# Attention prologue reordered: mask fill by token halves, layer norm of x in pairs, more v products before the first logits, four rotating PSUM banks

## The chip, the core and the metric

One core of one Trainium2 chip. TensorE is PE here, its weight loads PEld; VectorE is DVE, ScalarE ACT, GpSimd POOL, SyncE SP. DMAs are issued from the queues of SP, ACT and POOL, in the order in which those engines run their programs. The metric is the device time of one execution in microseconds, lower is better.

## The reference, cut to what matters

```python
def _A_ref(x, wqkv, wo):                      # B, S, D = 1, 2048, 576; H = 32 heads, Dh = 18
    qkv = (x @ wqkv).reshape(B, S, 3, H, Dh).transpose(2, 0, 3, 1, 4)
    q, k, v = qkv
    idx = pos[:, None] - (jnp.arange(8) * 2)[None, :]      # window of 8 keys, two tokens apart
    logits = einsum('bhsd,bhswd->bhsw', q, k[idx]) * Dh ** -0.5
    logits = where(idx >= 0, logits, -1e9)
    attn = softmax(logits)
    return einsum('bhsw,bhswd->bhsd', attn, v[idx]) (heads joined) @ wo

def _B_ref(x, w_in, w_sp, b_sp, w_out):       # F = 4608, gated with a 2048 x 2048 matrix over tokens
    z = gelu(x @ w_in); z1, z2 = halves of z; z2 = layernorm(z2)
    return (z1 * (w_sp @ z2 + b_sp)) @ w_out

x = x + _A_ref(layernorm(x), ...)             # layer 0
x = x + _B_ref(layernorm(x), ...)             # layer 1
x = x + _A_ref(layernorm(x), ...)             # layer 2
x = x + _B_ref(layernorm(x), ...)             # layer 3
```

## The kernel before, in words

The four layers run one after the other. The change touches the two attention layers (`layer_A`, li 0 and 2), above all what comes before their first logits. Inside `layer_A` the order of PE, ACT, DVE, POOL and SP is the order in which the program is written: each engine runs its instructions in that order, and so does each DMA queue.

**Layer norm and transposes of x (layer 0).** x is 16 tiles of 128 tokens. Statistics are three DVE instructions a tile (`LNX_stats`, L501 and L502), then epsilon is added (L504), POOL takes the power -1/2 (L505, called R here), and DVE applies it (L513). Tiles 0 to 3 are transposed on PE into `xnT` and copied by ACT (L520); tiles 4 to 15 by DMA transposes on SP (`ln_T`, L245). Statistics go by 2, 2, 2, 2, 4 and 4 tiles.

**Mask rows.** `QK` holds for each head 18 rows of q (index 0) and k (index 1) and 14 rows of a pattern that yields the window mask in the logits product: 128 partitions, four heads each, by 8 groups g of heads by 16 + 2048 tokens. `fill_window_rows` copies a pattern of 256 columns into all of it with DVE (L185, L187, L189), by pairs of groups.

**q and k (PG).** `PG(d, qk, cc)` is five matmuls (L383): seven heads (d = 0 to 3; four for d = 4), q or k, 512 tokens (cc). PSUM is copied to a staging tile `stg` by ACT (L355) or DVE (L353). When a staging tile is full (1024 tokens, q and k), one DMA for each head copies its 18 rows into `QK` (QK<-stg), dealt to the queues of POOL and SP by a fixed pattern (`queues`, 2 to 1). There are three staging tiles in layer 0, four in layer 2. Twenty PGs (cc = 0 and 1) come before the logits and four more (`pgs[:4]`) follow; 16 are spread over the steps.

**v (VW).** `VW(t, hh)` is five matmuls (L361) and one copy into `v_ext`, 19 columns a head, the last of which is 1. Six VW stand early in layer 0, two in layer 2; the others are spread over the steps.

**Steps.** Queries go in 19 tiles t of 112 tokens, each in two halves of 16 heads: step s = 2t + hf, 38 steps. Step s runs the logits of step s + 1 (`L_mm`, L407), the exponentials of s + 1 on ACT (`EXP`, L416), then PV(s) (L427) and DVE's division (L433, L434). After the second half the result is transposed into `oT` by a DMA on SP (L438). Logits need heads 0 to 15 in even steps, 16 to 31 in odd ones. A hand-written `table` adds to step s: PGs up to step 13 (`PG_END` = 14), VW(t) at 2t - 2 and 2t - 1, output projections `WO(i, hh)` (L453) at 2t + 4 and 2t + 5, where t is the last query tile that token tile i needs (2t + 3 at the end), the residual, statistics and normalisation of the result (`LN_XN` on POOL, L238), its transposes, and loads of the next layer's weights: `win2a` in six pieces from step 2 on, every second step, `win2b` in six pieces from step 16 on, every second step, both on POOL. `wo` is loaded on POOL at step 1 of layer 0.

**PSUM.** `H_tile` takes two times two banks for the logits. Of the other four banks `PT_tile` uses two (tag PT) and PV's result two (tag O); in layer B, with `any_bank`, tiles alternate between both tags.

Of the kernel before, what the change touches and what calls it, by code (L numbers as in the profile page):

```python
# [18 lines left out]
P = 128  # L19
# [43 lines left out]
class K:  # L63
# [24 lines left out]
    def setup(self):  # L88
# [18 lines left out]
        self.pt_rr = 0  # L107
# [8 lines left out]
    def build_window_rows(self, c):  # L116
# [8 lines left out]
        self.pat = self.consts.tile([P, 2, 256], bf16, name="win_pat")  # L125
# [43 lines left out]
        def load(eng):  # L169
            for j in range(4):  # L170
                self.dma(self.pat[32 * j + DH:32 * j + 32, :, :], one[:].rearrange("a r x -> r a x"), eng=eng)
# [10 lines left out]
    def fill_window_rows(self, QK, g0, g1):  # L182
        nc, S, n = self.nc, self.cfg.S, g1 - g0
        for a in range(2):
            nc.vector.tensor_copy(out=QK[:, a, g0:g1, 0:S].rearrange("p g (k x) -> p g k x", x=256),  # L185
                                  in_=self.pat[:, a, None, None, :].to_broadcast([P, n, S // 256, 256]))
            nc.vector.tensor_copy(out=QK[:, a, g0:g1, S:S + PADL],  # L187
                                  in_=self.pat[:, a, None, 0:PADL].to_broadcast([P, n, PADL]))
        nc.vector.tensor_copy(out=QK[:, 1, g0:g1, 0:PADL], in_=self.patpad[:, None, :].to_broadcast([P, n, PADL]))  # L189
# [4 lines left out]
    def PT_tile(self, shape, dt, name, any_bank=True):  # L194
        self.pt_rr += 1
        tag = "O" if any_bank and self.pt_rr % 2 else "PT"
        return self.ps.tile(shape, dt, name=name, tag=tag, bufs=2)

    def O_tile(self, shape, dt, name):
        return self.ps.tile(shape, dt, name=name, tag="O", bufs=2)  # L200
# [113 lines left out]
    def layer_A(self, li):  # L314
# [29 lines left out]
        def setup_bufs():  # L344
            for pb in P_bufs:
                nc.gpsimd.memset(pb[:, :, :, QT:P], 0.0)
            for ob_ in o_bufs:
                nc.gpsimd.memset(ob_[:, D:640], 0.0)
            nc.scalar.copy(out=v_ext[:, :, :, DH:DH + 1], in_=self.ones[:, None, None, :].to_broadcast([P, NT, H, 1]))
# [7 lines left out]
        def VW(t, hh, dve):  # L357
            nk = tdim(t)[0]
            pv = self.PT_tile([P, 512], f32, "pv", any_bank=False)
# [10 lines left out]
        def PG(d, qk, cc, dve, queues=(nc.sync, nc.gpsimd)):  # L370
# [8 lines left out]
            pp = self.PT_tile([P, 512], f32, "pp", any_bank=False)  # L379
# [39 lines left out]
        def PV(s):  # L419
            t, hf = divmod(s, 2)  # L420
            nk, nq = tdim(t)
            O_ps = self.O_tile([P, 512], f32, "O_ps")
# [23 lines left out]
        def WO(i, hh):  # L446
# [4 lines left out]
            pw = self.PT_tile([P, 512], f32, "pw", any_bank=False)  # L451
# [20 lines left out]
        if li == 0:  # L472
# [12 lines left out]
            self.load_wqk(nc.scalar)  # L485
            x_load(x1[:, 0:4, :], 4, 4, nc.sync)
            self.zero_right()
            self.build_window_rows(sb)
            self.load_pat(nc.sync)
            self.make_ident()  # L490
            warm = self.PT_tile([P, 512], f32, "warm", any_bank=False)
            for _ in range(40):
                nc.tensor.matmul(warm[:, 0:P], lhsT=self.ident[:], rhs=self.ident[:], start=True, stop=True)
            setup_bufs()

            def LNX_stats(i0, n):
                mv = sb.tile([P, 4, 2], f32, name="lnx_mv", tag="lnx_mv", bufs=2)
                for k_ in range(n):
                    st = sb.tile([P, 2, nc.vector.BN_STATS_DIM], f32, name="ln_st", tag="ln_st", bufs=3)
                    for s in range(2):  # L500
                        nc.vector.bn_stats(out=st[:, s, :], in_=xts[i0 + k_][:, s * 288:(s + 1) * 288])  # L501
                    nc.vector.bn_aggr(out=mv[:, k_, :], in_=st[:])  # L502
                rstd = sb.tile([P, 4], f32, name="lnx_rstd", tag="lnx_rstd", bufs=2)
                nc.vector.tensor_scalar_add(out=rstd[:, 0:n], in0=mv[:, 0:n, 1], scalar1=EPS)  # L504
                nc.gpsimd.tensor_tensor(out=rstd[:, 0:n], in0=rstd[:, 0:n], in1=self.neg_half[:, 0:1].to_broadcast([P, n]),  # L505
                                        op=ALU.pow)
                return i0, n, mv, rstd

            def LNX_apply(i0, n, mv, rstd, on_pe=False):
# [452 lines left out]
```

The softmax here doesn't subtract the row's maximum and nothing guards it: scores larger than these inputs give would overflow.

## Time and profile before

| what | us |
|---|---|
| median of 5 runs (1231.6 to 1240.11) | 1237.5 |
| the profiled execution | 1233.56 |
| its span, first to last instruction | 1231.8 |
| its mean granted TensorE clock | 0.993 |
| PE busy | 1194.5 |
| DVE / ACT / POOL busy | 545.3 / 385.0 / 275.7 |
| first 20 PGs of layer 0, first matmul | 15.95 |
| PV(0) of layer 0 | 55.06 |
| PV(0) of layer 2 | 658.70 |

The profile gives for one execution when each instruction ran, and for an idle engine what ended the wait (in brackets behind the row). A row of the windows gives, for a stretch of 5 us, the busy time and number of instructions of PE, PEld, DVE, ACT and POOL, then the granted PE clock (1.00 is full), the mean busy share of the 16 DMA engines and the GB/s moved. A row of the timeline gives start, duration, engine, line, operation, output <- input, and the number of instructions merged into it.

### The profile page before, as it was taken

Reading aid. Unit: us, or ns where it says so; the run is one execution under the profiler, and the core shown is the slowest. Engines: PE = TensorE matmul, PEld = TensorE weight load, DVE = VectorE, ACT = ScalarE, POOL = GpSimd, SP = SyncE. Lnnn points to the kernel's source line nnn. Section 1 sums busy time; section 2 is a strip of 40 time slices with the busy share of each in tenths; the row PEclk is TensorE's granted clock in tenths of the full one; section 3 lists DMA queues with packets and bytes.
Section 4 is the critical chain, followed back from the end, with each engine's and each line's share of the span. In section 5 each row is a group of like instructions: output and inputs, shape, how many; then the busy total and the mean of one; then the engine's idle time right before and its main releaser. Section 6 shows DMA issues by size and latency. Waiting matters only on the chain. (4 is left out here: it accounts for less than half of the span.)

```text
span 1231.8 us, 20796 instructions
## 1 busy us (share of the span) xinstructions
PE 1194.5 (97%) x8568; PEld 623.5 (51%) x8568; DVE 545.3 (44%) x1206; ACT 385.0 (31%) x605; POOL 275.7 (22%) x380
## 2 busy tenths in 40 slices
PE   7689999999999999999999999999999999999998
PEld 4256744444444444447754575444444444444577
DVE  8357867533332322334453676774332232332321
ACT  5357867501011011101146585772001101111000
POOL 3447677300000000001152576741000000000000
PEclk9899999999999999999999999999999999999999
DMA  6588989000000000046644898920000000000432
GB/s 178 108 167 191 191 164 193 22 1 11 11 11 12 1 11 11 1 154 191 173 103 109 181 223 173 241 58 22 1 11 11 11 11 11 12 1 2 135 109 73
DMA packets 176149, 101.58 MB, mean 82 GB/s; under 512 B 134954, under 2 KB 156506, under 8 KB 176054
## 3 DMA queue, kind: packets, MB, share of 16 engines
q1 hardware_dynamic: 163814, 76.04, 28.0%
q0 software_dynamic: 6896, 18.39, 5.9%
q10 hardware_dynamic: 5344, 5.83, 1.5%
q8 instruction: 67, 1.10, 0.4%
q14 instruction: 28, 0.23, 0.1%
HBM read 42.39 MB, written 16.53 MB: 48 GB/s over the span
## 5 line engine op out<-in xcount | busy, mean ns | idle before, releaser
L795 PE MATMUL pg<-Wq,Z 128*128 128x512 bf16 x2304 | 502.8, 379 | 0.0
L795 PEld LDWEIGHTS <-Z 128*128 128x128 bf16 x2304 | 225.7, 98 | 271.6
L799 DVE TENSOR_TENSOR g_tmp<-pg,ln_xn 128x512 f32<-128x512 f32 x144 | 99.6, 692 | 429.1 <-PE pg L795 429.1
L789 ACT ACTIVATE z1T<-pz 128x1024 bf16<-128x1024 f32 x72 | 73.7, 1023 | 513.9 <-PE pz L777 513.7
L849 PE MATMUL po<-wout,Z 128*128 128x288 bf16 x1152 | 141.4, 286 | 0.0
L77 POOL DMA_DIRECT2D wout<-in_B_w_out_dram x4 | 4.3, 1064 | 604.6 <-PE pg L795 604.6
L416 ACT ACTIVATE P_sb<-L_ps 128x896 bf16<-128x896 f32 (+1 forms) x152 | 126.4, 887 | 39.4 <-PE L_ps L407 38.9
L777 PE MATMUL pz<-xnT,w 128*128 128x512 bf16 (+1 forms) x640 | 136.0, 380 | 0.0
L849 PEld LDWEIGHTS <-Z 128*128 128x128 bf16 x1152 | 112.7, 98 | 28.8
L700 PEld LDWEIGHTS <-xnT 128*128 128x128 bf16 (+1 forms) x800 | 66.4, 97 | 82.2 <-issue 24.8
L383 PE MATMUL pp<-xnT,wqk_sb 128*128 128x512 bf16 x400 | 96.9, 392 | 8.7 <-ACT stg L355 5.3
L700 PE MATMUL pz<-win2a,xnT 128*128 128x512 bf16 x384 | 104.7, 381 | 0.0
L800 DVE TENSOR_TENSOR Z<-g_tmp,z1T 128x512 bf16<-128x512 f32 x144 | 99.7, 692 | 9.7
L777 PEld LDWEIGHTS <-w 128*128 128x128 bf16 (+1 forms) x640 | 51.1, 97 | 80.0 <-issue 27.1
L714 ACT ACTIVATE zp<-pz 128x1024 bf16<-128x1024 f32 x64 | 65.5, 1023 | 47.6 <-PE pz L700 32.3
L238 POOL TENSOR_SCALAR ln_xn<-x_new,ln_mv,ln_rstd 128x576 bf16<-128x576 f32 x32 | 73.3, 2290 | 3.4
L859 DVE TENSOR_TENSOR x_new<-po,xo 128x288 f32<-128x288 f32 (+1 forms) x64 | 28.8, 456 | 87.8 <-PE po L849 87.8
L700 PE MATMUL pz<-win2b,xnT 128*128 128x512 bf16 (+1 forms) x256 | 65.7, 380 | 0.0
L383 PEld LDWEIGHTS <-wqk_sb 128*128 128x128 bf16 x400 | 37.9, 100 | 53.1 <-issue 16.1
L77 POOL DMA_DIRECT2D QK<-stg x74 | 48.1, 653 | 64.4 <-ACT stg L355 17.2
L716 DVE CUSTOM_DVE_ANT_0 Z<-zp 128x1536 bf16<-128x1536 bf16 x32 | 57.1, 1783 | 11.3 <-ACT zp L714 11.3
L453 PE MATMUL pw<-wo_sb,oT 128*128 128x288 bf16 x320 | 50.2, 291 | 9.5 <-DVE stg L353 4.0
(103 smaller groups left out, 902.2 us busy)
## 6 DMA issues: line engine op xcount, KB each, us to landing
xres<-x_new SPq DMA_DIRECT2D x48, 288.0 KB
xo<-xres SPq DMA_DIRECT2D x48, 288.0 KB
QK<-stg POOLq DMA_DIRECT2D x74, 72.0 KB, 3.8
wout<-in_B_w_out_dram POOLq DMA_DIRECT2D x4, 1296.0 KB, 8.8
w<-in_B_w_in_dram SPq DMA_DIRECT2D x16, 256.0 KB
QK<-stg SPq DMA_DIRECT2D x54, 72.0 KB
win2a<-in_B_w_in_dram POOLq DMA_DIRECT2D x12, 288.0 KB, 4.2
wqk_sb<-in_A_wqkv_dram ACTq DMA_DIRECT2D x2, 1152.0 KB
```

The source lines that it names most:

```text
L238: e.tensor_scalar(out=xn[:nrows, 0:D], in0=x_t[:nrows, :], scalar1=mv[:nrows, 0:1], scalar2=rstd[:nrows, 0:1], op0=ALU.subtract, op1=ALU.mult)
L383: nc.tensor.matmul(pp[:, :], lhsT=w, rhs=self.xnT[:, c, PADL + cc * 512:PADL + (cc + 1) * 512], start=(c == 0), stop=(c == 4))
L416: nc.scalar.activation(out=P_bufs[(2 * s + jp) % 4][:nk, :, :, 0:nq], in_=Lv[:nk, :, :, 0:nq], func=ACT.Exp, scale=scale)
L700: nc.tensor.matmul(pzvs[ci][:, sub * 512:sub * 512 + w], lhsT=self.xnT[r0:r1, c, PADL + i * P:PADL + (i + 1) * P], rhs=win2(c)[r0:r1, c0 + ...
L714: nc.scalar.activation(out=zp[:, c0:c0 + cn], in_=pzvs[ci][:, 0:cn], func=ACT.Gelu_apprx_tanh, accum_out=sums[:, ci:ci + 1])
L716: nc.vector.tensor_tensor_reduce(out=spare[:, 0:SQ_D], in0=zp[:, 0:SQ_D], in1=zp[:, 0:SQ_D], scale=1.0, scalar=0.0, op0=ALU.mult, op1=ALU. ...
L777: nc.tensor.matmul(pz1s[q // 2][:, q % 2, :], lhsT=w1[r0:r1, c, sub * P:(sub + 1) * P], rhs=self.xnT[r0:r1, c, PADL + q * 512:PADL + (q + ...
L789: nc.scalar.activation(out=z1T[:, q2 * 512:(q2 + 2) * 512], in_=pz1s[q2 // 2][:, :, :].rearrange("p a b -> p (a b)"), func=ACT.Gelu_apprx_ ...
L795: nc.tensor.matmul(pg[:, :], lhsT=Z[:, jj, i, sub * P:(sub + 1) * P], rhs=Wq[q][:, i, :], start=(i == 0), stop=(i == NS - 1))
L799: nc.vector.tensor_tensor(out=tmp[:], in0=pg[:, :], in1=bsp[:, qs], op=ALU.add)
L800: nc.vector.tensor_tensor(out=uT(jj)[:, sub, qs], in0=tmp[:], in1=z1Ts[jj, sub][:, qs], op=ALU.mult)
L849: nc.tensor.matmul(acc[hh], lhsT=uT(j // 2)[:, j % 2, i * P:(i + 1) * P], rhs=wouts[j // NJH][:, j % NJH, hh * 288:(hh + 1) * 288], start= ...
```

## The change

- `PT_tile` has one tag with four banks for everything but the logits; `O_tile` is gone.
- The fill goes by token halves (columns 16 to 1039, then 1040 to 2063) and four groups at a time. Half 0 stands where the fill stood, half 1 after six pairs of PGs. The pattern tile is 16 columns wider, so that it can be read at an offset.
- Layer 0: statistics, epsilon, power and apply are separate helpers (`S_`, `E_`, `R_`, `A_`, `T_pe`, `T_`), and for tiles 0 to 7 they go in pairs with the v products in between. R for tiles 8 to 11 comes after the fifth pair of PGs, R for tiles 12 to 15 after the sixth, before half 1 and the apply.
- The ones of `v_ext` are a small ACT copy for t = 0 and a POOL memset for the others in layer 0, one POOL memset in layer 2. The load of wqk follows that ACT copy. `wo` is loaded in layer 0 right after the x loads. 26 warm-up matmuls, not 40.
- Eight VW more stand before the first logits in layer 0 (t = 3 to 6), six more in layer 2 (t = 1 to 3). Two PGs, not four, stand ahead of the steps, and they follow the first logits and have DVE copies; 18 go into steps 0 to 13.
- WO(0) to WO(2) of layer 0 come two steps later. `win2a` goes to steps 17, 19, ... 27.
- The head copies go to POOL and SP 5 to 2 in layer 0's first twenty PGs (`q3`), 1 to 1 in layer 2's. In layer 2 the first two PGs are copied by ACT.

```diff
@@ fill_window_rows
-        for a in range(2):
-            nc.vector.tensor_copy(out=QK[:, a, g0:g1, 0:S]..., in_=self.pat[:, a, None, None, :]...)
-            nc.vector.tensor_copy(out=QK[:, a, g0:g1, S:S + PADL], ...)
-        nc.vector.tensor_copy(out=QK[:, 1, g0:g1, 0:PADL], in_=self.patpad...)
+        if half == 0:
+            nc.vector.tensor_copy(out=self.pat[:, :, 256:272], in_=self.pat[:, :, 0:16])
+            nc.vector.tensor_copy(out=QK[:, 0, :, 0:PADL], ...)
+            nc.vector.tensor_copy(out=QK[:, 1, :, 0:PADL], in_=self.patpad...)
+        c0 = PADL + half * n
+        for g0 in (0, 4):
+            for a in range(2):
+                nc.vector.tensor_copy(out=QK[:, a, g0:g0 + 4, c0:c0 + n].rearrange("p g (k x) -> p g k x", x=256),
+                                      in_=self.pat[:, a, None, None, PADL:PADL + 256].to_broadcast([P, 4, n // 256, 256]))
@@ PT_tile
-        self.pt_rr += 1
-        tag = "O" if any_bank and self.pt_rr % 2 else "PT"
-        return self.ps.tile(shape, dt, name=name, tag=tag, bufs=2)
-    def O_tile(self, shape, dt, name):
-        return self.ps.tile(shape, dt, name=name, tag="O", bufs=2)
+        return self.ps.tile(shape, dt, name=name, tag="PT", bufs=4)
@@ layer_A, li == 0
-            self.load_wqk(nc.scalar)
             x_load(x1[:, 0:4, :], 4, 4, nc.sync)
             self.zero_right()
+            nc.scalar.copy(out=v_ext[:, 0, :, DH:DH + 1], in_=self.ones[:, None, :].to_broadcast([P, H, 1]))
+            self.load_wqk(nc.scalar)
 ...
-            for _ in range(40):
+            for _ in range(26):
                 nc.tensor.matmul(warm[:, 0:P], lhsT=self.ident[:], rhs=self.ident[:], start=True, stop=True)
-            st0 = LNX_stats(0, 2)
-            st1 = LNX_stats(2, 2)
-            LNX_apply(*st0, on_pe=True)
-            LNX_apply(*st1, on_pe=True)
-            for t in range(3):
-                for hh in range(2):
-                    VW(t, hh, False)
-            st0 = LNX_stats(4, 2)
-            st1 = LNX_stats(6, 2)
-            LNX_apply(*st0)
-            LNX_apply(*st1)
-            LNX_T()
+            S_(0, 1); E_(0, 2); R_(0, 2); S_(2); A_(0, 1); T_pe(0); T_pe(1)
+            VW(0, 0, False); VW(0, 1, False)
+            S_(3); E_(2, 2); R_(2, 2)
+            VW(1, 0, False); VW(1, 1, False)
+            S_(4); A_(2, 3); T_pe(2); T_pe(3); S_(5); E_(4, 2); R_(4, 2)
+            VW(2, 0, False); VW(2, 1, False)
+            S_(6); A_(4, 5); T_(4, 5); S_(7); E_(6, 2); R_(6, 2)
+            nc.gpsimd.memset(v_ext[:, 1:NT, :, DH:DH + 1], 1.0)
+            A_(6, 7); T_(6, 7)
             x_load(spare, 8, 4, nc.sync)
             x_load(...12, 4, nc.sync)
-            for g0 in range(0, 8, 2):
-                self.fill_window_rows(QK, g0, g0 + 2)
+            self.load_wo(nc.gpsimd)
+            self.fill_window_rows(QK, 0)
+            q3 = (nc.gpsimd, nc.gpsimd, nc.sync, nc.gpsimd, nc.gpsimd, nc.sync, nc.gpsimd)
             for k_, (d, cc) in enumerate(order):
                 for qk in (1, 0):
-                    PG(d, qk, cc, False, q2)
+                    PG(d, qk, cc, False, q3)
                 if k_ == 3:
-                    LNX_apply(*LNX_stats(8, 4))
+                    S_(8, 9, 10, 11); E_(8, 4)
                 if k_ == 4:
-                    LNX_T()
-                    LNX_apply(*LNX_stats(12, 4))
+                    R_(8, 4); A_(8, 9, 10, 11); T_(8, 9, 10, 11)
+                    S_(12, 13, 14, 15); E_(12, 4)
+                if k_ == 5:
+                    R_(12, 4)
+                    self.fill_window_rows(QK, 1)
+                    A_(12, 13, 14, 15)
                 if k_ == 7:
-                    LNX_T()
-            nvw = 3
+                    T_(12, 13, 14, 15)
+            nvw0, nvw = 3, 7
@@ layer_A, li == 2
-            q2 = (nc.gpsimd, nc.sync, nc.gpsimd)
+            q3 = (nc.gpsimd, nc.sync)
 ...
-                    PG(d, qk, cc, k_ == 0, q2)
+                    PG(d, qk, cc, False, q3)
                 if k_ == 0:
-                    for g0 in range(0, 8, 2):
-                        self.fill_window_rows(QK, g0, g0 + 2)
+                    self.fill_window_rows(QK, 0)
                     setup_bufs()
+                    nc.gpsimd.memset(v_ext[:, :, :, DH:DH + 1], 1.0)
 ...
+                if k_ == 5:
+                    self.fill_window_rows(QK, 1)
-            for hh in range(2):
-                VW(0, hh, hh == 0)
-            nvw = 1
+            nvw0, nvw = 0, 4
+        for t in range(nvw0, nvw):
             for hh in range(2):
+                VW(t, hh, False)
@@ the steps
-        for d, qk, cc in pgs[:4]:
-            PG(d, qk, cc, False, q2)
-        pgs = pgs[4:]
+        pre, pgs = pgs[:2], pgs[2:]
 ...
-            s = 2 * t + (4 if t < NT - 3 else 3)
+            s = 2 * t + (6 if li == 0 and i < 3 else 4 if t < NT - 3 else 3)
 ...
-        if li == 0:
-            at(1, self.load_wo, nc.gpsimd)
         for k_, f in enumerate(self.load_win2a(nc.gpsimd)):
-            at(2 + 2 * k_, f)
+            at(PG_END + 3 + 2 * k_, f)
 ...
         L_mm(0)
         EXP(0)
+        for d, qk, cc in pre:
+            PG(d, qk, cc, True, q2)
```

Calls that the change writes on lines of their own are joined with semicolons here.

## The prediction

> **What bounds it now.** I read the page's busy table first, then the windows of 5 us, the timeline of both attention layers and the chain of waits.
>
> ```profile
> PE 1194.5 (97%) x8568; PEld 623.5 (51%) x8568; DVE 545.3 (44%) x1206; ACT 385.0 (31%) x605; POOL 275.7 (22%) x380
> 50.00:55.00 5.00, 0.85 (x16) 0.48 (x15) 0.00 (x0) 2.86 (x4) 0.00 (x0) 0.88 0.62 108
> 55.00:60.00 5.00, 5.00 (x36) 1.90 (x38) 1.43 (x4) 0.92 (x1) 0.00 (x0) 0.50 0.00 0
> ```
>
> PE is busy 97%, so only work taken off PE's path, its idle time, or its slow clock can be won. The holes lie in layers 0 and 2 (attention). After the idle 50 to 55 us the granted clock is 0.50.
>
> What ends layer 0's hole (timeline; the first row from SP's own):
>
> ```profile
> 51.52 0.81 SPq L77 DMA_DIRECT2D QK<-stg  x1
> 54.86 0.28 PE L407 MATMUL L_ps<-QK 32*128 32x112 bf16 x2 [2.44 <-DMA QK<-stg]
> 55.06 0.60 PE L427 MATMUL O_ps<-v_ext,P_sb 128*128 128x19 bf16 x16
> 55.51 4.43 PE L383 MATMUL pp<-xnT,wqk_sb 128*128 128x512 bf16 x10
> ```
>
> One late head copy (SP, 51.52) releases the logits of step 1 at 54.86; PV(0) runs at 55.06, and the next ten matmuls take 4.43 us where ten take 2.32 at full clock.
>
> Later waits in the steps:
>
> ```profile
> 76.66 0.77 PE L453 MATMUL pw<-wo_sb,oT 128*128 128x288 bf16 x5 [2.26 <-issue]
> 78.14 3.78 PE L383 MATMUL pp<-xnT,wqk_sb 128*128 128x512 bf16 x10
> 93.68 0.77 PE L453 MATMUL pw<-wo_sb,oT 128*128 128x288 bf16 x5 [0.46 <-DVE stg L353]
> 628.87 19.87 PE L383 MATMUL pp<-xnT,wqk_sb 128*128 128x512 bf16 x90 [2.07 <-DVE stg L353]
> 659.15 3.41 PE L383 MATMUL pp<-xnT,wqk_sb 128*128 128x512 bf16 x10
> 728.46 0.79 PE L453 MATMUL pw<-wo_sb,oT 128*128 128x288 bf16 x5 [0.44 <-DMA oT<-o_t]
> ```
>
> Line 1: the first output projection waits 2.26 us, and line 2 pays for it in clock. Lines 3 and 4: PE waits for one of two PSUM banks. Line 5: slow clock again. Line 6 is the warning: in the dense steps oT's transpose is already a little late.
>
> Effective PE cost of a piece on the chain of waits: logits 0.33 to 0.48, PV 0.49, PG 1.11, VW 0.63, WO 0.61.
>
> **Layer 0 up to PV(0).** Until 26.7 us I expect nothing: the DVE still meets the x of tiles 4 to 7 at 12.05 (it idled 1.03 us for it), now with the applies of tiles 2 and 3 behind that wait, and four transposes on SP end near 22.3 as before (16.70 to 22.28). The mask fill keeps its eight large copies (1.22 each) and loses nine small ones; its first half ends about 5 us earlier on DVE (the groups that d=0 needs by 22.7), and the statistics of the pairs are as many as before. But the queue of POOL takes the 5 us: d=0's five copies (the first four took 2.89) 27.0 to 30.6, d=1's five (3.03) to 33.6, only then R(8..11), 1.03, to 34.6, against 33.4 before. Applies from 34.7; SP transposes 35.2 to 41.6 (6.45), then two copies each of d=2 and d=3 at 0.82 to 44.9. DVE: applies to 36.2, statistics 3.9 to 40.1, half fill 1 (4 x 1.22 = 4.9) to 45.0, first apply 45.4. Four transposes (6.70) 45.5 to 52.2, and behind them, on SP, the one copy of d=4. From issue to release 3.34 (51.52 to 54.86): 55.5. So PV(0) comes 0.7 us later. Bounds -2 (x lands earlier, since wqk is issued some 1.5 us later) to +3 (load_wo beside the transposes at 20 us). What d=2's earlier POOL copies (34.6 instead of 39.98) win is hidden behind this last copy. All else before PV(0) is free: 8 more VW fit into PE's wait, as do the first logits, the two early PGs and the memset of v_ext; if the cover went, the 8 VW would cost 5.0. The shorter warm-up (26 x 0.105 = 2.7 us, ending 8.4) costs nothing while the first transposes wait for DVE until about 8.6; the windows show clock 1.00 there.
>
> The Trainium skill ("TensorE: Matmul & The Clock Gate", Part 1) says that the clock opens only after about 3.4 us of activity, which speaks against cutting 4.19 us to 2.7: by it the ten transposes and first v products might run at half speed, an estimate of 1 to 2 us. By that rule up to 0.8 us could reach the chain to PV(0), and the sum would be -9.4. No run here shows a short warm-up yet.
>
> By the rows the sum keeps 0 for it: PE waited 1.21 us for the transposes at 23.79, which covers a slower start by so much.
>
> POOL's copies beside DVE fills: in layer 2, 14 took 11.83, 0.85 each, against a median of 0.593. Fill 1 lies beside eight copies of d=3 and d=4: 8 x 0.25 = 2 us, ending near 48, hidden by 55.5.
>
> **Layer 0, steps 0 to 13** (55.06 to 105.40 before).
> - Eight VW leave: 8 x 0.63 = -5.0.
> - Two more PGs inside (18, not 16): 2 x 1.11 = +2.2.
> - WO(0..2) two steps later, and win2a no longer beside them: step 6 took 5.57 where its pieces and bank wait give 3.3: -2.3; ten matmuls at 3.78 instead of 2.32: -1.4.
> - Bank waits: steps 9 to 13 average 3.58, their pieces 3.24; 0.34 x 7 = -2.4. In a ring of four each tile waits for one released a step before.
> - Sum -8.9. ACT (1.73 per step) stays below 2.0, the shortest new step.
>
> **Layer 2.** The half fill can start after the last statistics (626.2) instead of after the two casts (629.34), and d=0's copies go out near 630: no wait added. PE goes on at 626.8 instead of 628.87 (-2.07), since four banks hold two PGs more; 20 PGs end at 646.7; VW 8 x 0.71 to 652.4; logits; table load 1.28 and two exponentials 1.73 from 652.8 to 655.9, under which two PGs run; PV(0) at 656.3 instead of 658.70: -2.4. PE idles about 1 us instead of 3, so no slow clock: -1.1. Steps: six VW -3.8, two PGs +2.2, bank waits -2.4. WO(0) stays in step 6, and its transpose still queues behind head copies on SP (0.57 wait before, shorter steps now): +0.5. Sum -7.0. The ones on POOL instead of 2.84 us of ACT: hidden.
>
> **Dense steps (14 on).** win2a's six pieces per layer move from the PG phase into steps 17 to 27, between win2b's. On POOL: a tile costs 0.56+2.29+0.24 = 3.1, plus 2.29 steps x 0.62 = 1.4: 4.5 of 4.9 us, it still fits. On the DMA engines: the POOL queue moved 18.39 MB in 5.9% of 16 engines' span, so one 0.295 MB piece takes 1.17 us on all. oT's transpose took 5.63 us (722.78 to 728.41) with 0.44 of wait, among three win2b issues. Bounds per tile: 0 (layer 0 showed no wait at the same place) to 1.2; about five tiles a layer, so 0 to 12 us. I take 0.5 each: +5.0. Layer B: before, its PSUM tiles already alternated over the same four banks: 0.
>
> **Sum.** 0.7 - 8.9 - 7.0 + 5.0 = -10.2. The profiled execution took 1233.56 (span 1231.8 and 1.8 around it): 1223.4. The five timed runs go from 1231.6 to 1240.1 with the median 1237.5, 3.9 above the profiled execution; the mean of all six is 1235.5, 1.9 above it. I add 1.9: 1225.
>
> **Rivals.**
> 1. *Given back in the dense steps.* Each of ten tiles waits 1.0 to 1.2, about one more piece of 1.17 in each landing: -15.2 + 11 = -4.2, so 1231. For it: row 728.46, and DMA shares near 1. Against it: windows after win2b's end (135 to 150 us) show the same shares, 0.78 to 1.17, without a wait.
> 2. *The ring does not help.* If each tile's bank is still held by a late evacuation (DVE in order behind a half fill or statistics), 2 x 2.4 + 2.07 = 6.9 is lost: 1232. Against: steps 14 on use three tiles a step, DVE lags under one step.
> 3. *Slower.* One mechanism: with win2a and win2b in every step, the transposes of oT land as late as at the worst place before, and one piece later. In step 6 of layer 0 the transpose issued at 69.53 was followed by its reader at 76.66, 7.1 us later, with two win2a pieces and wo in flight; 7.1 + 1.2 = 8.3 against a slack of 5.63 - 0.44 = 5.2 is a wait of 3.1 per tile. Ten tiles: 31, sum -15.2 + 31 = +15.8: 1251. It decides from 1.5 us per tile (15.2 / 10). Against: that transpose queued behind four head copies on SP, and none are left in steps 17 to 27.
> 4. *The prologue is shorter than I think*: the chain to PV(0) ends 3 us earlier and no tile waits: 1217.
>
> **Chances.** Forecast (1218 to 1231) 0.55, rival 1 0.14, rival 2 0.08, rival 3 0.10, rival 4 0.13. About 0.5%, 6 us, is what a measurement can tell from no change: faster means below 1231.3. Rivals 1 and 2 lie on that border, and I count a tenth of their 0.22 as faster. Faster 0.55 + 0.13 + 0.02 = 0.70, same 0.20, slower 0.10. Range: rival 4 less 3, to rival 2 plus 5, about the spread of single runs round their mean (1231.6 and 1240.1 round 1235.5): 1214 to 1237.
>
> **What would show it.** Right: PV(0) of layer 0 at 54 to 58, its release still a head copy behind four transposes; steps 0 to 13 near 41 to 42 us; no 2.07 wait in layer 2 and PV(0) some 32 us after its first PG (34.2 before); no "DVE stg" wait at WO. Wrong: WO waits of over 1 us on oT in steps 17 to 29; PV(0) beyond 59; steps 0 to 13 above 47 us.

## The result, and the profile after

The changed kernel is slower: 1242.72 us (median of 24 runs, 1236.44 to 1249.28) against 1236.94 beside it on the same chips, a ratio of 1.005 (95% interval 1.0037 to 1.0063). The forecast was 1225. The difference is about as large as a measurement of this kernel can tell; the interval does not contain 1, so a small loss is clear, but not its exact size. The profiled execution took 1244.26 us, its span is 1242.5, 10.7 more than before.

Cut at the same events, the two spans compare so (us; each from the starts of the named matmuls in PE's timeline):

| stretch | before | after | change | predicted |
|---|---|---|---|---|
| layer 0, start to PV(0) | 55.1 | 60.6 | +5.5 | +0.7 |
| layer 0, PV(0) to PV(14) | 50.3 | 41.7 | -8.6 | -8.9 |
| layer 0, PV(14) to layer 1's first matmul | 47.6 | 58.7 | +11.1 | +2.5 |
| layer 1 | 471.5 | 472.0 | +0.6 | 0 |
| layer 2, first PG to PV(0) | 34.2 | 35.9 | +1.6 | -2.4 |
| layer 2, PV(0) to PV(14) | 47.1 | 41.6 | -5.6 | -4.6 with the clock |
| layer 2, PV(14) to layer 3's first matmul | 48.5 | 53.4 | +4.9 | +2.5 |
| the rest | 477.4 | 478.6 | +1.1 | 0 |

The steps in which the gain was looked for gave it, 14.2 us in the two layers. The prologues and the dense steps took 23.2.

The busy table and the windows at the end of layer 0's prologue, the columns as before:

```profile
PE 1199.2 (97%) x8554; PEld 624.5 (50%) x8554; DVE 549.1 (44%) x1193; ACT 377.4 (30%) x599; POOL 279.8 (23%) x379
```
```profile
50.00:55.00 5.00, 2.52 (x16) 0.98 (x14) 2.20 (x6) 1.57 (x2) 3.21 (x6) 1.00 1.03 137
55.00:60.00 5.00, 0.27 (x1) 0.10 (x1) 0.00 (x0) 0.00 (x0) 0.00 (x0) 0.51 0.95 129
60.00:65.00 5.00, 4.89 (x35) 2.08 (x35) 1.41 (x3) 1.73 (x2) 0.00 (x0) 0.50 0.00 0
```

PE is busier by 4.7 us with 14 warm-up matmuls fewer: the mean clock fell from 0.993 to 0.986. The empty window before PV(0) is still there, one window later, with the 0.50 clock behind it. The timeline shows the same release as before, five microseconds late (SP's own row first):

```profile
56.48 0.81 SPq L77 DMA_DIRECT2D QK<-stg  x1
60.11 0.56 PE L403 MATMUL L_ps<-QK 32*128 32x112 bf16 x9 [2.28 <-DMA QK<-stg]
60.59 0.60 PE L423 MATMUL O_ps<-v_ext,P_sb 128*128 128x19 bf16 x16
61.04 4.41 PE L379 MATMUL pp<-xnT,wqk_sb 128*128 128x512 bf16 x10
```

The rows that stand where the later waits of before stood:

```profile
84.04 0.78 PE L449 MATMUL pw<-wo_sb,oT 128*128 128x288 bf16 x5
641.10 19.11 PE L379 MATMUL pp<-xnT,wqk_sb 128*128 128x512 bf16 x80 [3.54 <-ACT stg L351]
669.37 2.32 PE L379 MATMUL pp<-xnT,wqk_sb 128*128 128x512 bf16 x10
731.87 1.35 PE L449 MATMUL pw<-wo_sb,oT 128*128 128x288 bf16 x5 [3.46 <-issue]
```

The first output projection waits for nothing now. No PSUM wait on `stg` stands before an output projection in steps 0 to 13. In layer 2 the ten matmuls after PV(0) run at full clock. But the 2.07 us wait in layer 2's first PGs has become 3.54, on ACT and not on DVE, and the warning of 0.44 us at oT has become 3.46 (the row names no releaser; the transpose of oT that it reads is looked at below), with the slow clock behind it (1.35 instead of 0.78 for five matmuls).

The chain of waits through layer 0's prologue names the first loss; under it, PE's row of that place before the change:

```profile
18.76 2.46 issue
21.22 0.57 DVE ln_xn L514
...
22.62 4.79 DMA xnT<-ln_xn
...
27.54 17.06 PE pp L379 x70
```
```profile
23.79 8.79 PE L383 MATMUL pp<-xnT,wqk_sb 128*128 128x512 bf16 x40 [1.21 <-DMA xnT<-ln_xn]
```

The chain finds 2.46 us on DVE in which it waits for nothing that the profile shows; they lie inside one apply. The last transpose then needs 4.79 us to land, so that PE goes on at 27.54, after a wait of 4.86 us, instead of 23.79. In the timeline, POOL's and DVE's rows of that moment lie on each other (two applies take 0.72 us at 13.14):

```profile
18.54 2.60 POOL L557 MEMSET v_ext<- 128x576 bf16 x1
18.63 3.16 DVE L514 TENSOR_SCALAR ln_xn<-x_in,lnx_mv,lnx_rstd 128x576 bf16<-128x576 bf16 x2 [0.81 <-POOL lnx_rstd L506]
```

### The profile page after: what moved, and what is told of

Its sections match the earlier page's. It is cut to its first block, busy times and chain, and to the rows that moved or that the text cites. A ratio compares the mean times of both kernels' runs of the same rounds, so it can differ in the third digit from the quotient of the medians.

```text
span 1242.5 us, 20721 instructions
## 1 busy us (share of the span) xinstructions
PE 1199.2 (97%) x8554; PEld 624.5 (50%) x8554; DVE 549.1 (44%) x1193; ACT 377.4 (30%) x599; POOL 279.8 (23%) x379
## 4 chain that ended last, share of the span: by engine, by line
PE 92%; DMA 4%; DVE 1%; issue 1%; SPq 1%; POOL 1%; ACT 1%; DVEq 0%; POOLq 0%
PE pg L824 40%; PE pz L806 12%; PE po L878 11%; PE pz L729 10%; PE pp L379 6%; PE pv L357 3%; PE pw L449 3%; PE O_ps L423 2%; PE L_ps L403 2%; DMA oT<-o_t 2%; PE pzs L729 1%; DMA x_in<-in_A_x_dram 1%; DMA xres<-x_new 1%; SPq L242 0%; DMA xnT<-ln_xn 0%
## 5 line engine op out<-in xcount | busy, mean ns | idle before, releaser
L745 DVE CUSTOM_DVE_ANT_0 Z<-zp 128x1536 bf16<-128x1536 bf16 x32 | 56.6, 1770 | 13.1 <-ACT zp L743 13.0
L357 PE MATMUL pv<-wv_sb,xnT 128*128 128x288 bf16 (+1 forms) x380 | 58.2, 293 | 3.4 <-DVE o_t L430 1.4
```

The costliest lines, as they stand in the source:

```text
L357: nc.tensor.matmul(pv[:nk, 0:288], lhsT=self.xnT[:, c, QT * t:QT * t + nk], rhs=wv_sb[:, c, hh * 288:(hh + 1) * 288], start=(c == 0), stop ...
```

## The experiments

All times are medians, ratios are to the kernel before beside it on the same chip, with the 95% interval. The kernel before had medians from 1235.6 to 1236.9 beside the different runs, so a difference of two medians is good to about 1 us; the ratios are free of that. The other columns give what one profiled execution of each kernel shows in the stretches that matter (us). For "wo in step 1" (1251.2) and "ones, wo behind d = 0" (1243.1) it was the slowest of twelve, so their late stretches may be worse than typical.

| kernel | time | ratio | PV(0), layer 0 | layer 0: steps 0-13 | 14-19 | 20-25 | layer 2: first PG to PV(0) | 20-25 |
|---|---|---|---|---|---|---|---|---|
| before | 1236.9 | 1 | 55.1 | 50.3 | 12.9 | 12.4 | 34.2 | 13.0 |
| changed | 1242.7 | 1.005 (1.004, 1.006) | 60.6 | 41.7 | 18.3 | 17.3 | 35.9 | 18.2 |
| ones on ACT | 1243.0 | 1.006 (1.004, 1.008) | 59.5 | 41.7 | 17.6 | 18.5 | 34.2 | 22.5 |
| wo in step 1 | 1244.0 | 1.006 (1.003, 1.009) | 61.5 | 41.3 | 18.5 | 19.0 | 35.5 | 26.3 |
| ones, wo behind d = 0 | 1237.2 | 1.002 (0.999, 1.004) | 56.3 | 41.7 | 17.8 | 19.4 | 37.0 | 17.6 |
| projections back | 1236.4 | 0.999 (0.997, 1.002) | 59.8 | 40.2 | 13.3 | 17.3 | 35.5 | 19.4 |
| seven projections later | 1234.9 | 0.999 (0.997, 1.002) | 60.5 | 38.5 | 12.9 | 13.1 | 36.9 | 20.4 |
| four x_new | 1242.2 | 1.005 (1.003, 1.007) | 61.3 | 40.8 | 18.6 | 16.9 | 35.8 | 18.7 |
| win2a back | 1238.3 | 1.002 (0.999, 1.004) | 59.8 | 42.4 | 18.4 | 16.4 | 37.0 | 15.5 |
| projections and win2a back | 1230.2 | 0.995 (0.992, 0.997) | 60.8 | 40.6 | 16.3 | 12.4 | 37.1 | 13.9 |
| layer 2's PGs on DVE | 1237.8 | 1.003 (1.001, 1.005) | 59.9 | 41.8 | 18.2 | 19.4 | 30.6 | 13.0 |
| before, ring only | 1227.2 | 0.993 (0.991, 0.995) | 55.1 | 47.5 | 12.9 | 15.2 | 32.7 | 12.5 |
| five edits | 1220.8 | 0.987 (0.985, 0.989) | 56.9 | 40.6 | 14.8 | 13.2 | 30.8 | 13.7 |
| five, pow sooner | 1222.1 | 0.988 (0.986, 0.991) | 55.6 | 41.1 | 15.9 | 12.4 | 31.1 | 13.6 |
| five, win2b thinner | 1220.2 | 0.987 (0.984, 0.990) | 55.9 | 39.5 | 14.4 | 13.9 | 30.9 | 15.1 |
| five and both | 1221.5 | 0.986 (0.983, 0.990) | 58.0 | 40.4 | 14.3 | 13.2 | 30.9 | 13.5 |
| five, v back in the steps | 1224.0 | 0.990 (0.987, 0.994) | 57.2 | 44.4 | 13.3 | 13.8 | 27.6 | 17.0 |

### Layer 0's prologue: the memset and wo

```diff
-            nc.gpsimd.memset(v_ext[:, 1:NT, :, DH:DH + 1], 1.0)
+            nc.scalar.copy(out=v_ext[:, 1:NT, :, DH:DH + 1], ...ones...)      # right after load_wqk
```

> The ones of v_ext in layer 0 written by one ACT copy ahead of everything else ACT does there, instead of POOL's memset (2.60 us at 18.54) beside DVE's applies of tiles 6 and 7 (3.16 us for two at 18.63; two elsewhere 0.72). Theory A, the memset stretches the applies and with them the whole chain to the first PV: the applies take 0.7 us, the four transposes of tiles 4 to 7 end 2 to 2.5 us sooner, the first PV comes at 58.0 to 58.6 instead of 60.59, and the time falls by 2 to 2.5 us, to some 1240.5. Theory B, the transposes and head copies are late for what they share with loads (wo, x), not for the applies: the applies are short, but the first PV stays within 0.6 us of 60.6, and so does the time.

The apply fell to 0.97 us (timeline, DVE), so the memset did stretch it. But PE still waited 4.36 us for xnT, PV(0) came only 1.1 us sooner (no more than the spread of the seven kernels with the changed prologue as it is, 59.8 to 61.3), and the time did not move. Theory A was right about the apply and wrong about the price: another cause stood behind it.

```diff
-            self.load_wo(nc.gpsimd)                # after the x loads
+        if li == 0:
+            at(1, self.load_wo, nc.gpsimd)
```

> wo loaded in step 1 again, as before the change, and nothing else undone. Theory A, the wo load (issued at 20.7, with x at 24.0 and 24.6) slows the transposes of tiles 4 to 7 that are in flight: PE's wait for them (4.86 us at 27.54) falls by 1 to 2 us, the first PV comes at 58.8 to 59.6, the steps stay as they are, since the first output projection now comes in step 8: the time falls by 1 to 2 us. Theory B, the transposes are late only because the applies ahead of them are: PE's wait stays within 0.4 us of 4.86, the time is unchanged within 0.6 us.

PE's timeline, and POOL's row of the wo load:

```profile
24.78 17.10 PE L379 MATMUL pp<-xnT,wqk_sb 128*128 128x512 bf16 x70 [2.68 <-DMA xnT<-ln_xn]
...
61.02 0.56 PE L403 MATMUL L_ps<-QK 32*128 32x112 bf16 x9 [5.77 <-DMA QK<-stg]
```
```profile
50.55 1.38 POOL L77 DMA_DIRECT2D wo_sb<-in_A_wo_dram  x2
```

The wait for the transposes fell by 2.2 us, as theory A has it. Then the load, which before the change waited until 63.62 behind head copies on POOL, went out at 50.55 and was in flight with the last head copies: from SP's issue at 53.83 to the release 7.2 us instead of 3.6. In this profile the gain was lost at the other end, which neither theory said. So both were taken away in one kernel, wo going out between the head copies of d = 0 and d = 1:

```diff
+                if k_ == 3:
+                    self.load_wo(nc.gpsimd)        # and the ones on ACT as above
```

> Layer 0's prologue with the ones on ACT and the wo load issued on POOL behind the head copies of d=0, so that neither the memset nor wo lies beside the transposes of tiles 4 to 7. Alone, the ones on ACT shortened the applies from 3.16 to 0.97 us but PE still waited 4.36 us for xnT; wo moved to step 1 cut that wait to 2.68 but met the last head copies (5.77 us). Theory A, the two delays stand in series, and with both away PE goes on 3.5 to 4.5 us sooner than in the changed kernel (23.0 to 24.0 instead of 27.54) and the first PV comes at 56.0 to 57.5 instead of 60.59; the time falls by 3 to 4.5 us. Theory B, what comes after (the statistics' pow behind ten head copies on POOL) sets the first PV, and the earlier xnT is lost there: first PV at 58.5 or later, the time 0 to 2 us shorter.

```profile
23.87 15.57 PE L379 MATMUL pp<-xnT,wqk_sb 128*128 128x512 bf16 x70 [1.59 <-DMA xnT<-ln_xn]
...
55.77 0.56 PE L403 MATMUL L_ps<-QK 32*128 32x112 bf16 x9 [2.76 <-DMA QK<-stg]
```

PE goes on 3.7 us sooner, the first PV comes at 56.3, 4.3 us sooner, and the time falls by 5.5 us by the medians, 4.3 by the ratios: theory A. The kernels below that have both edits too show the first PV at 55.6 to 58.0, those without either at 59.8 to 61.3. Of the +5.5 in the first row of the first table, 4.3 were the memset and the wo load; taking away one of them alone gained nothing in the time.

### Steps 14 to 19 of layer 0: a bunch of output projections

```diff
-            s = 2 * t + (6 if li == 0 and i < 3 else 4 if t < NT - 3 else 3)
+            s = 2 * t + (4 if t < NT - 3 else 3)
```

> The first three output projections of layer 0 back in the steps where they were before the change (6, 8, 10 instead of 8, 10, 12). Theory A, the shift puts four of them into steps 12 to 14, where the three x_new buffers run out, DVE waits for stores (3.67, 1.87 and 2.74 us), and PE behind it for a PSUM bank: these waits fall under 0.5 us each, the six steps after step 14 take 14 to 15 us instead of 18.3, the first output projection waits 0 to 2.3 us again in step 6; net 2 to 4 us faster. Theory B, the stores land late for what else is on the DMA engines: waits of 1.5 us and over remain, the six steps stay above 17 us, and the time is unchanged or up to 2 us longer.

The three DVE waits for stores are gone and steps 14 to 19 take 13.3 us: theory A, with 6.4 us instead of 2 to 4. DVE's rows in the changed kernel, with PE's two rows that wait for the banks behind them:

```profile
100.78 0.46 DVE L452 TENSOR_TENSOR x_new<-pw,xo 128x288 f32<-128x288 f32 x1 [3.67 <-DMA xres<-x_new]
108.44 0.46 DVE L452 TENSOR_TENSOR x_new<-pw,xo 128x288 f32<-128x288 f32 x1 [1.87 <-DMA xres<-x_new]
114.84 0.46 DVE L452 TENSOR_TENSOR x_new<-pw,xo 128x288 f32<-128x288 f32 x1 [2.74 <-DMA xres<-x_new]
```
```profile
108.95 0.55 PE L423 MATMUL O_ps<-v_ext,P_sb 128*128 128x19 bf16 x16 [0.97 <-DVE x_new L452]
115.35 0.77 PE L357 MATMUL pv<-wv_sb,xnT 128*128 128x288 bf16 x5 [1.34 <-DVE x_new L452]
```

The shift moves tiles 0, 1 and 2 to steps 8, 10 and 12, but tile 3 has step 12 already, and tile 4 step 14. Is the shortage of x_new buffers the cause, or the bunch?

```diff
-                st["x"] = sb.tile([P, D], f32, name="x_new", tag="x_new", bufs=3)
+                st["x"] = sb.tile([P, D], f32, name="x_new", tag="x_new", bufs=4)
```

> The changed kernel with four x_new buffers instead of three, nothing else. Theory A, with the projections of tiles 2, 3 and 4 pushed together DVE runs out of x_new buffers and waits for stores (3.67, 1.87, 2.74 us), PE then for a bank that DVE has not read: with one more buffer these waits go, steps 14 to 20 of layer 0 take 13 to 14 us instead of 18.3, the time falls by 3 to 5 us. Theory B, the stores and transposes are late for the crowd itself and the next thing late stops PE (the transpose of oT, POOL's layer norm): steps 14 to 20 stay above 16 us, the time falls by under 2 us.

```profile
115.43 1.38 PE L449 MATMUL pw<-wo_sb,oT 128*128 128x288 bf16 x5 [2.59 <-DMA oT<-o_t]
```

Theory B. DVE no longer waits for a store, and the same steps take 18.6 us: PE now stops at the transpose of oT. The buffer was only the first to be late. Left was whether the later place as such is bad. Shifting seven tiles puts them at steps 8, 10, ... 20, and tile 7 stands at 22 anyway, so no step has two:

```diff
-            s = 2 * t + (6 if li == 0 and i < 3 else 4 if t < NT - 3 else 3)
+            s = 2 * t + (6 if li == 0 and i < 7 else 4 if t < NT - 3 else 3)
```

> The changed kernel with the first seven output projections of layer 0 two steps later instead of the first three: tiles 0 to 6 then start in steps 8, 10, 12, 14, 16, 18 and 20, tile 7 in 22, and no two in the same step (with three, tiles 2 and 3 both start in step 12). Theory A, the bunch makes stores and transposes late: steps 14 to 20 take 13 to 14.5 us instead of 18.3, the time falls by 3 to 6 us, to 1237 to 1240. Theory B, the later place as such does it (the tail of each tile runs beside win2b and win2a): steps 14 to 20 stay above 16.5 us, the time within 2 us of 1242.7.

Steps 14 to 19 take 12.9 us and steps 20 to 25 take 13.1, and the time is 1234.9: theory A, and more than it asked. The bunch was the cause of the 18.3. The later place as such does no harm: the ratio is that of the kernel with the projections back. Steps 0 to 13 take 38.5 us, the shortest of all, but two half projections have left them for later steps. A wait of 2.65 us for oT is left at 137.60, in step 30.

### The dense steps: win2a beside win2b

```diff
-            at(PG_END + 3 + 2 * k_, f)
+            at(2 + 2 * k_, f)
```

> The six win2a pieces of each attention layer back in steps 2 to 12, where they were before the change, instead of 17 to 27. Theory A, win2a beside win2b makes the transposes of oT land late: the waits of 1.27 to 3.46 us for oT after step 17 in both layers go below 0.6, the time from step 14 to the feed-forward's first matmul falls from 58.7 towards 53 us in layer 0 and from 53.4 towards 49 in layer 2, steps 0 to 13 grow by 0 to 2 us a layer; net 5 to 9 us faster, level with the kernel before or better. Theory B, the oT waits come from the four output projections bunched in steps 12 to 14, and go on from there: layer 2, which has no bunch, gains 0 to 2 us, layer 0 nothing; net within 2 us of unchanged.

The time fell by 4.4 us, and layer 2, which has no bunch, gained 2.7 of them after step 14 (53.4 to 50.7): between the theories, since one wait of 1.73 us for oT stayed there. Layer 0, which still has the bunch, gained 1.5 (58.7 to 57.2). With the projections back as well:

> Both at once: the first three output projections of layer 0 and the win2a pieces where they were before the change (alone, 6.4 and 4.4 us faster than the changed kernel). Theory A, two separate causes, DVE's wait for the stores in steps 12 to 19 and late transposes of oT in steps 20 to 25: the gains add up, steps 14 to 20 take 13 us, steps 20 to 26 13 to 15 in both layers, the time falls to 1231 to 1234, below the kernel before by 3 to 6 us. Theory B, one cause, too much on the DMA engines after step 14, which either edit relieves: the second edit adds under 1.5 us, 1235 to 1237. With both back, steps 0 to 13 of layer 0 must show whether win2a beside the first output projections costs there (2.26 us of wait in step 6 before the change).

1230.2 us, 12.5 below the changed kernel, where the two alone make 10.8: theory A in the time, two causes that add up. Steps 20 to 25 take 12.4 and 13.9 us. But steps 14 to 19 of layer 0 take 16.3 and not the 13 of theory A, with a wait for oT in step 16 that neither edit alone shows:

```profile
108.93 0.79 PE L449 MATMUL pw<-wo_sb,oT 128*128 128x288 bf16 x5 [2.06 <-DMA oT<-o_t]
```

The transpose that it reads was issued on SP at 100.92, half a microsecond after the last win2a piece on POOL (100.36). Four of the five kernels further down that have both edits wait at the same place, 1.2 to 1.6 us. The earlier win2a makes late transposes rarer, but does not end them.

In layer 2, one profile each, the eight kernels with win2a in steps 17 to 27 took 13.0 to 26.3 us for steps 20 to 25 (mean 19.5; the one with 13.0 has its late transpose in the next six steps, 17.7), the seven built on the changed kernel with win2a in steps 2 to 12 took 13.5 to 17.0 (mean 14.6). Without a wait they take 12.9. Not every late transpose has win2a beside it: the ring by itself (below), with win2a in its old place, has a wait of 2.60 us for oT in layer 0's step 24. How it looks in the changed kernel, on POOL and on SP (each from its own rows):

```profile
724.34 0.61 POOL L77 DMA_DIRECT2D win2b<-in_B_w_in_dram  x1
725.50 0.58 POOL L77 DMA_DIRECT2D win2a<-in_B_w_in_dram  x1
```
```profile
723.71 3.15 SPq L434 DMA_TRANSPOSE oT<-o_t  x1
```

Two pieces leave while the transpose is being issued, and each took 5.8 us to land. The transpose, whose issue takes 1.2 us elsewhere, has taken 3.15 on SP's queue, and the projection that reads it starts at 731.87, 8.2 us after the issue began (5.6 before the change). That is one place; that the pieces delay the transpose is carried by the two groups of kernels, not by these rows.

### Layer 2's prologue

```diff
-                    PG(d, qk, cc, False, q3)
+                    PG(d, qk, cc, k_ == 0, q3)
```

> The first two PGs of layer 2 evacuated by DVE again, so that the mask fill waits for them on DVE as before the change. Theory A, the eight fill copies that now run in one piece (9.56 us) slow POOL's small operations (2.36 and 2.18 instead of 0.55 and 0.26 us), ACT's last layer norm waits 7.28 us for them and PE 3.54 us for ACT: with the fill behind the two casts these POOL operations take 0.6 and 0.3 us again, the 3.54 us wait and the slow clock after it go, from the first PG to the first PV it takes 32 to 33.5 us instead of 35.9, and the time falls by 2 to 4 us, to 1239 to 1240.5. Theory B, 20 PGs, 8 v products and the exponentials set that stretch whatever ACT does: it stays above 35 us, the time within 1 us.

The timeline of the changed kernel at the start of layer 2:

```profile
634.86 9.56 DVE L190 COPY QK<-win_pat 128x4096 bf16<-128x4096 bf16 x8
634.89 2.36 POOL L216 TENSOR_TENSOR ln_rstd<-ln_rstd,neg_half 128x1 f32<-128x1 f32 x1 [3.50 <-DVE ln_rstd L215]
637.35 2.18 POOL L220 TENSOR_SCALAR ln_nmr<-ln_mv,ln_rstd 128x1 f32<-128x1 f32 x1
...
639.57 0.87 ACT L229 ACTIVATE ln_xn<-x_new,ln_nmr,ln_rstd 128x576 bf16<-128x576 f32 x1 [7.28 <-POOL ln_nmr L220]
```

and with the one edit (POOL's rows, then PE's):

```profile
636.09 0.55 POOL L216 TENSOR_TENSOR ln_rstd<-ln_rstd,neg_half 128x1 f32<-128x1 f32 x1 [3.50 <-DVE ln_rstd L215]
636.73 0.27 POOL L220 TENSOR_SCALAR ln_nmr<-ln_mv,ln_rstd 128x1 f32<-128x1 f32 x1
```
```profile
634.28 21.88 PE L379 MATMUL pp<-xnT,wqk_sb 128*128 128x512 bf16 x100
```

All 100 matmuls of the twenty PGs run in one piece, PV(0) comes 30.6 us after the first PG (30.6 to 31.1 in the five kernels with this edit and as many early v products, 34.2 to 37.1 in the changed kernel and the eight built on it without the edit), and the time falls by 4.9 by the medians, 3.1 by the ratios: theory A. The two DVE casts were what held the fill back until POOL had done its two small operations. POOL's P_sb memsets, 3.86 us under the fill, take 0.64 again.

That agrees with the Trainium skill, "SBUF — State Buffer", section "Who interferes with whom": a DVE copy in a two-port mode and a GpSimd operation exclude each other for a whole instruction, and the one that comes second blocks. The durations here (2.36 and 2.18 against 0.55 and 0.27, each about as long as two fill copies of 1.2) and the 2.46 us that DVE stood still beside the memset fit that in both directions; no run here shows which mode DVE was in.

### The ring by itself

```diff
-        self.pt_rr += 1
-        tag = "O" if any_bank and self.pt_rr % 2 else "PT"
-        return self.ps.tile(shape, dt, name=name, tag=tag, bufs=2)
+        return self.ps.tile(shape, dt, name=name, tag="PT", bufs=4)        # and O_tile the same
```

> The kernel before with nothing but the ring of four banks instead of two pairs. Theory A (the prediction's terms): the bank waits of steps 0 to 13 go (2.4 us a layer) and the 2.07 us wait in layer 2's first PGs, in all 5 to 7 us: 1230 to 1232. Theory B, a tile that takes its bank from the common ring waits for the slowest of its neighbours in turn, and the waits only change their place: 1235 to 1238.

1227.2 us: theory A, with more than its upper end by the medians. In the one profile steps 0 to 13 lose 2.8 us in layer 0 and 1.8 in layer 2, and layer 2's stretch up to PV(0) 1.5. This one part of the change would have beaten the kernel before by 0.7%.

### All mendings together

The five edits are the ones above: ones on ACT, wo behind d = 0, projections back, win2a back, layer 2's first PGs on DVE.

> Five edits of the changed kernel at once: ones on ACT, wo behind the head copies of d=0, the first three output projections and win2a where they were before the change, layer 2's first two PGs on DVE. Alone or in pairs they measured 1242.98 (ones), 1237.2 (ones and wo), 1230.2 (projections and win2a), 1237.8 (layer 2), against 1242.7 for the changed kernel. Theory A, the delays of the two prologues are in series with those of the later steps: the gains add up to 5.5 + 12.5 + 4.9 = 23 us, less what later waits give back, 1220 to 1225, below the kernel before by 11 to 16 us. Theory B, a steadier PE meets the DMA engines sooner and the transposes of oT give half back: 1226 to 1230.

1220.8 us, 0.987 (0.985 to 0.989) of the kernel before and 21.9 below the changed one: theory A. That is below the 1225 of the forecast, but with five parts of the change taken back or replaced. From its page, cores apart:

```profile
PE 1189.0 (97%) x8554; PEld 620.7 (51%) x8554; DVE 549.2 (45%) x1195; ACT 378.5 (31%) x598; POOL 274.2 (22%) x378
```

PE is busy 10.2 us less than in the changed kernel with as many matmuls: the clock (0.996 against 0.986 in the mean). Three variations, the first `R_(8, 4)` after the fourth pair of PGs, the second `at(PG_END + 2 + 3 * k_, win2b_piece, k_)`, the third both. ("The fourth run's kernel" in the first text is the one with the ones on ACT and wo behind d = 0.)

> The five edits, and layer 0's pow of tiles 8 to 11 issued on POOL one pair of head projections sooner, so that it no longer queues behind ten head copies (34.73 with DVE waiting for it in the fourth run's kernel). Theory A, the applies, the four transposes, the statistics of tiles 12 to 15 and so the last head copy come some 2 us sooner: first PV of layer 0 at 54 to 55, 1.5 to 2 us off the time of the five edits. Theory B, PE's own work up to the first logits (70 matmuls, 40 of v) or the transposes' order on SP holds the end: first PV within 0.7 us of the five edits.

> The five edits with the six win2b pieces three steps apart instead of two (steps 16 to 31 instead of 16 to 26). Theory A, the waits for oT that are left (1 to 2.6 us at one or two places) come from win2b pieces beside the transposes, and a thinner stream of them avoids it: no wait for oT over 1 us before step 32, 1 to 4 us off the time of the five edits. Theory B, a transpose is late when one piece happens to fall on it, and the spacing only moves the place: within 1.5 us of the five edits.

> The five edits with both additions: the pow of tiles 8 to 11 one pair sooner, the win2b pieces three steps apart. Theory A, the first PV of layer 0 at 55.0 to 55.9 and one oT wait fewer a layer: 1216 to 1219. Theory B, each was within 1.5 us of the five edits and their sum is too: 1219 to 1222.

1222.1, 1220.2 and 1221.5: theory B each time in the time. In the first the PV(0) came 1.2 us sooner, at 55.6, but in the second, without the earlier pow, it came at 55.9, and in the third, with it, at 58.0: no gain from the pow is shown. In the second there are waits for oT of 1.37, 1.38, 1.57 and 2.56 us, in other places than with two steps' spacing. What is gained or lost there is below what these runs can tell apart.

Last, the v products:

```diff
-            nvw0, nvw = 3, 7
+            nvw0, nvw = 3, 3
 ...
-            nvw0, nvw = 0, 4
+            nvw0, nvw = 0, 1
```

> The five edits, but with the v products ahead of the first logits as few as before the change (three pairs in layer 0, one in layer 2), the other 14 back in the steps. Theory A (the prediction's terms), they lie in PE's waits in layer 0's prologue, where they cost nothing, and in layer 2 they only change place: 8 x 0.63 = 5 us longer in layer 0, up to 1 us in layer 2: 1224 to 1227 against 1220.8. Theory B, the steps of layer 0 have slack for them since the ring of four banks took PE's waits away, or the logits come sooner without them: within 1.5 us of the five edits.

1224.0, 3.2 us more than the five edits, though the intervals of the two ratios overlap. The stretch is clearer: steps 0 to 13 of layer 0 take 44.4 instead of 40.6 (39.5 to 41.1 in the four kernels with the five edits), and PV(0) comes no sooner: 3.8 us, near the 5.0 of theory A. In layer 2 PV(0) comes 3.2 us sooner without them and the steps take 2.2 more: about even.

## Why the prediction was wrong

The sum was -10.2, the spans differ by +10.7. Of the 21 us between, 4.8 are layer 0's first PV, 4.0 layer 2's first PV and 11.0 the dense steps; the steps 0 to 13 came out nearly as summed.

**Layer 0's first PV (+0.7, bounds -2 to +3; measured +5.5).** The step that failed is "all else before PV(0) is free". POOL's memset was put beside work in the sum and nothing was asked of what DVE does in that moment; it does the applies that the chain passes through. The wo load was seen, as the reason for the upper bound of +3, and not in the value. The two together are 4.3. That x would land sooner because wqk is issued later fell too: wqk went out at 1.93 (1.87 before) and DVE's wait for x ended at 12.16 (12.05 before). The structure was right: R behind ten head copies, four transposes, one last head copy. With the memset and the wo load out of the way, R starts at 34.73 (33.6 in the prediction, without a wo load of 1.38 ahead of it) and PV(0) at 56.3.

**Steps 0 to 13 of layer 0 (-8.9; -8.6).** Right in the sum, and in two parts that were tried: v products 3.8 of 5.0, the ring 2.8 of 2.4. The -3.7 for the later projections and win2a was not earned by moving them. With both back in their old places the changed kernel has no wait in step 6 and takes 40.6 us for these steps, 1.1 less than with them moved (in the five edits' profile a wait of 1.20 us stands there). The ring alone, by contrast, still waits 2.51 us in step 6. So something else in the change took that wait away; the wo load, which now goes out before the steps and not at 63.62, and the two PGs fewer ahead of them are candidates that no run separates. For this term the sum was right by luck.

**The projections' shift, its price in no term.** The prediction counted what leaves step 6 (-3.7 with the clock) and did not write down the steps of the tiles that follow. Tile 3 stays at step 12. The loss of 5.4 us in steps 14 to 19 is the largest that was not in the working at all, and the seven-tile shift shows that it need not have come.

**Layer 2's first PV (-2.4; measured +1.6).** The failed step is "the half fill can start after the last statistics: no wait added". It may start then, but so do POOL's two small operations, on which ACT's last layer norm waits, and behind it in ACT's order the casts of the first PGs, and behind them PE. The prediction had used the slowing of POOL's copies beside fills (0.85 against 0.593) as a price of 0.25 us each, a mean over queue entries, and never set it against POOL's arithmetic. The ring's part of the reason held: with the casts back on DVE the wait is zero and the stretch is 3.6 us shorter than before, with six v products more in it.

**Steps 0 to 13 of layer 2 (-4.6 from its parts, the clock's 1.1 among them; -5.6).** Right, too small by 1.0; the term of +0.5 for the transpose behind head copies did not come.

**Dense steps (+5.0, bounds 0 to 12; measured +16.0).** The bunch makes 5.4 of it (layer 0's steps 14 to 19). The rest, between 10 and 11, is within the bounds but twice the value, and about what rival 1 put there (11). The price was spread as 0.5 us over ten tiles. The trace has one or two tiles a layer that wait 1.3 to 3.5 us, and a slow clock behind some of them that costs up to as much again (5.3 us in steps 20 to 25 of layer 2 for one wait of 3.46). Rival 3's mechanism was there, at a third of its price of 31: by itself it would have left the sum at -15.2 + 10, so the sign came from the bunch and the two prologues.

**Rivals 2 and 4.** Rival 2 fell by the ring alone (0.993). Rival 4's prologue came the other way.

**The warm-up of 26.** The trace does show a price:

```profile
8.51 1.25 PE L521 MATMUL pt<-ident,ln_xn 128*128 128x128 bf16 x10
13.57 0.79 PE L521 MATMUL pt<-ident,ln_xn 128*128 128x128 bf16 x10 [0.63 <-DVE ln_xn L514]
```

The first ten transposes, behind a warm-up of 2.96 us, take 1.25 us, the next ten 0.79, as the first ten did before the change. That fits the rule of the Trainium skill ("TensorE: Matmul & The Clock Gate", Part 1) that the prediction left out of its sum. The clock of 1.00 that it read there settles nothing: the windows of the changed kernel read 1.00 from 8 to 10 us too. The first PG starts at 16.05 against 15.95, and PE waits 4.86 us further on, so nothing of it reached PV(0). In the profiles of the five edits and of the pow sooner the same ten take 0.85 and 0.77, so the price is not paid in every execution.

## What to carry to other kernels

Before an operation on an idle engine is called free, look at what the other engines do in that very moment, and at who waits for them: a memset on POOL cost DVE 2.4 us on the chain, and a fill on DVE cost PE 3.5 us by way of POOL and ACT. When a few members of a regular schedule are moved, write down the steps of those that are not, and look for two in one place. And when two delays stand in series, undoing either may show nothing: the ones alone and the wo load alone gave no gain, together 5.5 us by the medians.

## What the runs showed that was not expected

A wait of PE for oT may or may not be followed by the slow clock, and its length alone does not tell. After 1.57 and 1.73 us in two of the kernels the next five matmuls took 1.38 us. After 2.60 us with the ring alone the clock stayed at 1.00 for the 6 us that follow. After 2.65 us in the kernel with seven projections later the next five matmuls took 0.79, but five of the next step took 1.41, so the slow clock can also come late. The windows of the kernel with win2a back (its wait of 1.73 us ended at 733.27) show it:

```profile
732.00:734.00 2.00, 0.73 (x4) 0.46 (x5) 0.61 (x2) 0.07 (x1) 1.89 (x2) 0.82 1.36 159
734.00:736.00 2.00, 2.00 (x38) 1.19 (x37) 0.71 (x2) 0.76 (x1) 1.46 (x3) 0.50 1.07 309
736.00:738.00 2.00, 2.00 (x35) 1.33 (x34) 0.93 (x3) 1.42 (x4) 0.00 (x0) 0.82 0.60 176
```

PE is busy all the time from 734 on, and by the three rows works at half its clock for about 3.4 us (an estimate: 0.7 + 2.0 + 0.7). What decides between the two is open. The late transposes themselves also differ from kernel to kernel where the code of the layer is the same: in layer 2's steps 20 to 25, 17.6, 18.2, 18.7, 19.4, 20.4, 22.5 and 26.3 us for seven kernels that differ only in layer 0 or in a buffer. One profile tells that a transpose will be late, not which and by how much.
